# Float32 fillers and a new order for all 780 tasks of a fused attention and maxout kernel

## The chip, the cores and the metric

One core of a Trainium2 chip runs the whole program. The metric is the device time of one execution in microseconds (us). Of the core's engines, PE (TensorE) does the matrix products, DVE (VectorE), ACT (ScalarE) and POOL (GpSimd) do element-wise work, and SP (SyncE) issues DMAs. Each engine works through its own instructions strictly in the order in which the program lists them, and waits at semaphores for the others.

## The reference

Attention with B=4, H=8, S=768, D=64, followed by a maxout layer:

```python
k_sum = k.reshape(B, H, nb, 32, D).max(axis=3)        # nb = 24 blocks of 32
v_sum = v.reshape(B, H, nb, 32, D).mean(axis=3)
scores_l = scale * q @ k.T                            # kept where |i - j| < 16
scores_s = scale * q @ k_sum.T + log(32)
a = softmax(concat(masked scores_l, scores_s))
attn = a @ concat(v, v_sum)                           # (B, H, S, D)
x = attn.transpose(0, 2, 1, 3).reshape(3072, 512)
out = maximum(x @ w1, x @ w2) @ w_out                 # w1, w2: 512 x 1024; w_out: 1024 x 512
```

All inputs and the output are float32 in HBM.

## The kernel before

**Algebra.** max(h1, h2) = h1 + relu(h2 - h1). So the kernel forms `wd` = w2 - w1 and `w1o` = w1 @ w_out, and computes out = x @ w1o + relu(x @ wd) @ w_out. Products are in bfloat16.

**Work units.** A task is a short run of instructions on one engine. There are 780. Names carry the batch b, the head pair hp (0 to 3, two heads each) and the group grp (0 to 2, 256 query rows each). In order of data flow:

- `load kb·hp`, `load qb·hp`, `load vb·hp`: one DMA each from SP (`load_kq`, `load_v`); `load w0` to `load w3` (two DMAs each: one piece of w1 and of w2) and `load wo0` to `load wo3`. They land in a ring of 13 buffers (`land`).
- `cast k`, `cast q`, `cast v`: float32 to bfloat16, on DVE, ACT or POOL (`copy`, line 593). `turn k`, `turn q`: transpose on PE (line 624), or by DMA (line 628) for the pairs 22, 23, 30 to 33. `place`: out of PSUM. `max k`: block maximum (line 650, DVE). `wrap`, `tails`, `sums k`: the window's neighbours and the block maxima put beside the keys.
- `hide` (a mask product, line 690, batch 0 only), `scores` (line 701), `exp` (ACT, line 715), `mask` (DVE, line 725, batches 1 to 3), `values` (lines 757 and 762), `inv` and `x` (DVE, lines 813 and 816), then `xt`: x transposed, on PE plus a copy for batch 0 (lines 831 and 593), by a DMA of SP for the others (line 822).
- `odd v`, `sums`, `all sums`: v shifted by 64 rows, and the block means of v copied where `values` reads them.
- `wd 0` to `wd 3` (line 856): w2 - w1, on DVE or POOL; `w1b`, `turn w1`, `w1t`: w1 transposed for `w1o` (line 897).
- `hidden b·grp·n` (line 913, eight 128x256 products each, n = 0 to 3), `relu` (lines 922 and 924), and `out b·grp·u` (first part line 940, two more parts line 947), `copy out` and `store` (line 958). `hidden` with n odd reads wd 1 and wd 3; with n even it reads wd 0 and wd 2.
- `warm` (line 982): products that nobody reads, into a free PSUM bank; 14 of them fill PE's time while the first loads arrive. Each is two 128x512 bfloat16 products of the constant `identity`, which a DVE copy makes (line 328) from the float32 constant `ident32` of POOL.

**What sets the order.** `Plan.given` takes three lists of the constant `CFG` and does no planning: `order` (the task numbers in program order), `engines` (a letter for each task: T for PE, D, A, P, S) and `slots` (which buffer of its ring each new tile takes). The prices handed to `op` are therefore not used at run time. PSUM is one ring of eight banks; a task that takes a bank waits for the last reader of what was in it.

**Batches overlap.** PE works on `hidden` and `out` of one batch between the pieces of the next batch's attention. In batch 0 there is no earlier batch, so until `wd` is there PE has only the attention of batch 0 and the fillers.

Of the kernel before, what the change touches and what calls it, by code (L numbers as in the profile page):

```python
# [56 lines left out]
""".split()))  # L57
CFG["engines"] = "".join("""
PDPPPDDDPAPDPDDDDPTTTTTTTTTTTTTTSSSAAAATDDPPSSSADPATAAPPSSSPDDPTADDDSSSPDDPTADDPSSDPTASSPATDSSDATDSSPATASDSASASDDTDTAD
PPPDDTDTADPDADDTATDDPDDDPTATDDPPDDTTATDDTDTTATDDTDTTATDDTDTTATDDTDTTATDDTATTATDDTDSSSPSSSPSSSDSSSPPADAPDDDTAPDPAAPDPAT  # L60
DTDDADDDPTATDDPADDTADTDDSTADTDDSTADTDDSATPTADADADDTDTDDADAATADTDDSTADTDDSTADTDDSSSSPSSSASSSASSSPPDAPDDPPTDPPPAAAPPATDT
ADPAAAATPTADPPPDTADTDDSTADTDDSTADTDDSPSPSDDPAAASASDDPPPTADTDDSTADTDDSTADTDDSSSSPSSSPSSSASSSPPDAPDDPDTAPADPPPPPASPSDDAD
PDSDSDDPPDTADTDDSTADTDDSTADTDDSASPSADAADPSDSADAPDTADTDDSTADTDDSTADTDDSTTATTATTDTTDTDTATDTATTTDSTTTDSTATATATATTTAATTTAS
TATATDTDTTTASTTTDSTDTATDTDTTTDATTTDSTDTATATDTTTDATTTASTATDTATATTTDSTTTDSTATDTATATTTDATTTAATDTATATATTTASTTTASTATATATATT
TDSTTTAATDTDTDTDTTTDSTTTDATDTATDTDTTTDATTTASTATDTDTATTTAATTTDSTTTDSTTTAA
""".split())
# [58 lines left out]
class Task:  # L125
    NEVER = 10 ** 9
    done, start = NEVER, None
# [107 lines left out]
def kernel(  # L235
# [39 lines left out]
    def bank(buf, n=512, dt=F32, second=0):  # L275
        a = bank_tile[:, buf.ap + second]
        return (a if dt is F32 else a.bitcast(BF16))[:, 0:n]
# [782 lines left out]
```

## Time and profile before

| | |
|---|---|
| runs | 167.3, 166.43, 167.31 us (median 167.3) |
| profiled execution | 166.2 us, its span 164.4 us |
| PE busy | 153.0 us of the span (93%) |
| DVE, ACT, POOL busy | 113.0, 92.9, 57.8 us |
| `warm` products | 28, 8.7 us of PE's busy time |
| HBM | 25.17 MB read, 6.29 MB written |

The span runs from the first to the last instruction of the program; the execution's own time is 1.8 us longer. Rows of the timeline give the start, the length, the engine, the line, output and inputs, and how many instructions were merged; in square brackets stands the idle time of the engine before them and what ended it. A matmul's recorded end is modelled and holds some 0.16 us of pipeline after its last column, so the pace of PE is read from start to start. Some matmul records are missing.

### The profile page before, as it was taken

What the parts mean: (1) busy time and instruction counts of PE and PEld (TensorE: products, weight loads), DVE (VectorE), ACT (ScalarE), POOL (GpSimd) and SP (SyncE); (2) the same over time, 40 slices, a digit from 0 to 9 for tenths busy, and PEclk for the clock granted to TensorE, in tenths of its full rate; (3) what the DMA queues carried; (4) which work ended last, traced back from release to release, by engine and by line L of the source; (5) the groups of instructions that cost most, each with busy time, mean ns of one, the idle gap of its engine ahead of it and who ended that gap; (6) DMA issues with size and microseconds to landing.
All of it is one profiled execution on the core that took longest, in us unless ns stands there. A gap on an engine that the chain in (4) does not pass through costs nothing.

```text
span 164.4 us, 4431 instructions
## 1 busy us (share of the span) xinstructions
PE 153.0 (93%) x1793; PEld 100.2 (61%) x1812; DVE 113.0 (69%) x224; ACT 92.9 (57%) x134; POOL 57.8 (35%) x91
## 2 busy tenths in 40 slices
PE   5889978999999999999999999999899999999992
PEld 2346657998565644575687646678545467766651
DVE  3698898579856899994989986569746654163221
ACT  3469995794577698836996645283937312012010
POOL 6058757302242385534672546034630000000000
PEclk9999999999999999999999999999999999999999
DMA  5999999999999999999979997997999996311015
GB/s 157 289 331 303 273 386 383 383 382 371 274 190 289 271 233 219 130 232 136 201 169 229 228 209 162 121 261 150 220 245 335 319 174 167 58 64 70 0 66 189
DMA packets 67700, 36.46 MB, mean 222 GB/s; under 512 B 54624, under 2 KB 61664, under 8 KB 67680
## 3 DMA queue, kind: packets, MB, share of 16 engines
q1 hardware_dynamic: 66208, 33.76, 87.6%
q10 hardware_dynamic: 1472, 2.43, 4.4%
q8 instruction: 14, 0.23, 0.6%
q14 instruction: 6, 0.05, 0.1%
HBM read 25.17 MB, written 6.29 MB: 191 GB/s over the span
## 4 chain that ended last, share of the span: by engine, by line
PE 62%; DMA 14%; DVE 11%; issue 4%; SPq 4%; ACT 2%; POOL 1%; ACTq 0%; POOLq 0%; DVEq 0%
PE banks L913 19%; PE banks L947 17%; PE banks L940 10%; DMA land<-in_k_dram 8%; DMA out_dram<-o 6%; PE banks L897 4%; PE banks L624 3%; PE banks L757 3%; DVE vx L593 3%; PE banks L701 2%; PE banks L982 2%; DVE ks L650 2%; DVE pb L725 2%; DVE kqb L593 1%; SPq L428 1%
## 5 line engine op out<-in xcount | busy, mean ns | idle before, releaser
L913 PE MATMUL banks<-xt,wd 128*128 128x256 bf16 x384 | 45.9, 273 | 0.1
L947 PE MATMUL banks<-wo,g 128*128 128x512 bf16 (+2 forms) x194 | 43.4, 362 | 1.8 <-issue 1.6
L913 PEld LDWEIGHTS <-wd 128*128 128x128 bf16 x384 | 37.3, 98 | 7.8 <-issue 0.5
L947 PEld LDWEIGHTS <-g 128*128 128x128 bf16 x208 | 18.7, 98 | 17.3
L715 ACT ACTIVATE pb<-banks 128x1024 bf16<-128x1024 f32 x24 | 23.6, 1026 | 6.2 <-PE banks L701 3.8
L940 PE MATMUL banks<-w1o,xt 128*128 128x512 bf16 (+2 forms) x100 | 23.5, 362 | 0.2
L922 ACT ACTIVATE g<-banks 128x512 bf16<-128x512 f32 x27 | 15.2, 604 | 7.6 <-PE banks L913 7.6
L924 DVE TENSOR_SCALAR g<-banks 128x512 bf16<-128x512 f32 x21 | 14.1, 686 | 7.8 <-PE banks L913 7.6
L816 DVE TENSOR_TENSOR xs<-banks,inv 128x512 bf16<-128x512 f32 x24 | 16.0, 686 | 4.9 <-DMA xt<-xs 4.4
L593 POOL COPY vx<-sums 32x792 bf16<-32x792 bf16 x15 | 14.7, 983 | 12.5 <-ACT sums L593 7.0
L725 DVE TENSOR_TENSOR pb<-pb,mask 128x1024 bf16<-128x1024 bf16 (+1 forms) x24 | 16.4, 710 | 4.0 <-ACT pb L715 3.7
L593 ACT COPY o<-banks 128x512 f32<-128x512 f32 (+1 forms) x8 | 4.4, 546 | 25.6 <-PE banks L947 21.1
L593 POOL CAST kqb<-land 128x768 bf16<-128x768 f32 x9 | 8.9, 985 | 20.1 <-DMA land<-in_q_dram 9.8
L940 PEld LDWEIGHTS <-xt 128*128 128x128 bf16 x104 | 9.9, 98 | 9.4
L650 DVE TENSOR_REDUCE ks<-kx 128x24 bf16<-128x768 bf16 x16 | 15.0, 945 | 0.2
L593 DVE COPY o<-banks 128x512 f32<-128x512 f32 (+2 forms) x10 | 6.2, 621 | 10.2 <-PE banks L947 8.7
L593 POOL CAST vx<-land 128x768 bf16<-128x768 f32 x10 | 8.9, 889 | 10.2 <-DMA land<-in_v_dram 10.2
L593 ACT CAST kqb<-land 128x768 bf16<-128x768 f32 x11 | 10.3, 943 | 3.2 <-DMA land<-in_k_dram 2.5
L593 DVE CAST kqb<-land 128x768 bf16<-128x768 f32 x12 | 7.0, 590 | 7.1 <-DMA land<-in_k_dram 4.7
L624 PE MATMUL banks<-ident,kqb 128*128 128x128 f32 x60 | 9.7, 278 | 1.4 <-DVE kqb L593 1.1
L757 PEld LDWEIGHTS <-pb 128*64 128x64 bf16 (+1 forms) x384 | 8.0, 110 | 4.9 <-issue 2.8
L757 PE MATMUL banks<-vx,pb 128*64 128x65 bf16 (+1 forms) x384 | 9.5, 196 | 1.3 <-DVE xs L816 0.8
(87 smaller groups left out, 183.1 us busy)
## 6 DMA issues: line engine op xcount, KB each, us to landing
land<-in_k_dram SPq DMA_DIRECT2D x16, 384.0 KB, 6.0
land<-in_v_dram SPq DMA_DIRECT2D x16, 384.0 KB, 6.9
land<-in_q_dram SPq DMA_DIRECT2D x16, 384.0 KB, 5.9
land<-in_moe_w_dram SPq DMA_DIRECT2D x8, 512.0 KB, 9.6
land<-in_moe_w_out_dram SPq DMA_DIRECT2D x4, 512.0 KB, 10.0
out_dram<-o SPq DMA_DIRECT2D x7, 256.0 KB, 4.0
out_dram<-o ACTq DMA_DIRECT2D x4, 256.0 KB, 2.8
out_dram<-w1t SPq DMA_DIRECT2D x3, 256.0 KB, 3.4
```

The lines of the kernel that those rows point to most:

```text
L593: {"D": nc.vector.tensor_copy, "A": nc.scalar.copy, "P": nc.gpsimd.tensor_copy}[e](out=o, in_=i)
L624: nc.tensor.transpose(out=bank(ps)[:, 128 * j:128 * j + 128], in_=src.ap[:].bitcast(F32)[:, 128 * j:128 * j + 128], identity=ident32[:])
L650: op("D", 0.95, lambda e: nc.vector.tensor_reduce(out=ks.ap[:, 0:nb], in_=free(kt(), 128, [256, NM], [192, 2], [32, 2], [1, 32]), axis=AX. ...
L715: op("A", {"A": 1.03}, lambda e: nc.scalar.activation(out=spread(pb.ap[:, 0, 0:1], [192, 8], [128, 2], [1, 64]) if PW > 128 else spread(pb ...
L725: nc.vector.tensor_tensor(out=o, in0=o, in1=spread(mask[:, 2 * u:2 * u + 1, 0:1], [0, n], [64, 2], [1, 64]), op=ALU.mult)
L757: nc.tensor.matmul(out=o, lhsT=p[r], rhs=vx[b].ap[r, par, hp + n, 2 * grp + u, a, 0:D + 1], start=(PW == 128 or par == 0), stop=(last and ...
L816: op("D", 0.69, lambda e: nc.vector.tensor_tensor(out=x.ap[:].rearrange("p n u a d -> p n (u a) d"), in0=spread(bank_tile[:, ps.ap, 0:1], ...
L913: nc.tensor.matmul(out=bank(ps)[:, 256 * s:256 * s + 256], lhsT=wd_tile[:, quarter, c, 128 * s:128 * s + 128], rhs=x.ap[:, c, :], start=(c ...
L922: nc.scalar.activation(out=o, in_=bank(ps), func=ACT.Relu)
L924: nc.vector.tensor_scalar_max(out=o, in0=bank(ps), scalar1=0.0)
L940: nc.tensor.matmul(out=bank(ps, c1 - c0), lhsT=x.ap[:, c, sl], rhs=w1o[c].ap[:, cols], start=(c == 0), stop=False)
L947: nc.tensor.matmul(out=bank(ps, c1 - c0), lhsT=g.ap[:, f, sl], rhs=wo[f // 2].ap[:, f % 2, cols], start=False, stop=(f == FC - 1))
```

## The change

1. A filler becomes one 128x256 float32 product of `ident32`.
2. `order`, `engines` and `slots` are replaced as a whole. The tasks and what they compute stay the same, 185 of the 780 change their engine, and nearly all change their place.
3. One price of the planner (ACT's cast) is 1.0 instead of 1.06; nothing at run time reads it.

```diff
 CFG["order"] = list(map(int, """
-44 32 2 0 3 10 12 1 4 6 11 15 13 8 112 20 30 26 56 25 46 113 116 9 122 7 123 126 14 47 16 117 34 118 132 168 28 23 133
...
+44 22 20 26 19 0 5 10 3 9 32 4 56 1 6 11 12 13 112 34 18 113 132 122 116 118 7 15 117 45 46 68 14 33 31 133 123 27 25
...
 CFG["engines"] = "".join("""
-PDPPPDDDPAPDPDDDDPTTTTTTTTTTTTTTSSSAAAATDDPPSSSADPATAAPPSSSPDDPTADDDSSSPDDPTADDPSSDPTASSPATDSSDATDSSPATASDSASASDDTDTAD
...
+PDPDDPPPDDPPDPPPPPTTTTTTTTTTTTTTSSSPPADTDAPDSSSADADTDDDDSSSPDDDTADDDSSSPDPPTAADDSSPPTASSPATDSSDATASSPATDSPSPSDSDATDTDD
...
 CFG["slots"] = list(map(int, """
-0 1 0 0 0 0 0 0 0 0 0 0 1 0 2 1 3 0 0 0 1 1 1 0 0 0 0 0 4 0 0 2 4 0 0 0 1 5 2 0 0 0 0 0 2 0 0 1 4 1 0 1 4 1 0 0 0 0 0
...
+0 0 1 0 1 0 0 0 0 1 2 0 0 0 0 0 3 0 0 1 2 0 0 0 0 0 4 5 6 0 0 1 1 2 0 3 1 0 0 0 0 0 0 0 0 1 0 1 0 2 4 0 2 3 6 0 3 0 0
...
-            copy(eng, {"D": 0.58, "A": 0.84 if by_dma else 1.06, "P": 0.83 if by_dma else 1.05}, cast, by_engine=True,
+            copy(eng, {"D": 0.58, "A": 0.84 if by_dma else 1.0, "P": 0.83 if by_dma else 1.05}, cast, by_engine=True,
...
-            for _ in range(2):
-                nc.tensor.matmul(out=bank(ps), lhsT=identity[:], rhs=spread(identity[:, 0:1], [0, 4], [1, 128]),
-                                 start=True, stop=True)
+            nc.tensor.matmul(out=bank(ps, 256), lhsT=ident32[:], rhs=spread(ident32[:, 0:1], [0, 2], [1, 128]),
+                             start=True, stop=True)
```

The lists read out, for the stretches that matter below ("x2" is a repeat):

| list | before | after |
|---|---|---|
| PE, up to the first `hidden` | warm x4, turn k00, k01, hide 001, warm x2, turn k02, warm x3, sums 02, warm x3, sums 00, warm, turn q01 ... turn w1 1, x000, x001, x020, x021, k12, then hidden 023 | warm x5, turn k00, warm, turn k02, k01, warm x4, hide 001, turn q01, sums 00, warm, sums 02, warm, turn q00, warm, turn k03, scores 001, warm ... turn w1 3, x020, x001, w1 1, then hidden 003 |
| PE, up to the first `hidden` with n even | hidden 023, 003, 021, turn w1 2, hidden 011, turn w1 0, turn k10, hidden 013, 001, then 022 | hidden 003, 001, turn x021, k12, hidden 023, 013, turn w1 0, hidden 011, 021, turn k10, turn w1 2, then 002 |
| SP, weights | w3 x2, w1 x2, k12, w2, w0, k10, w0, w2, wo1, k13, k11, wo0, wo2, wo3 | w3 x2, w1 x2, k12, k10, w0 x2, w2 x2, wo0, k11, wo1, wo2, k13, wo3 |
| engine of wd 0, 1, 2, 3 | DVE, POOL, DVE, POOL | POOL, POOL, DVE, POOL |
| PE, batch 1 into 2 | ... scores 100, values 102, 101, out ... hidden 113, 110, 111, 112, out x3, turn q20, hidden 120, out x2, scores 201, 200 | ... scores 100, out x2, turn q21, out, values 101, 102, out ... hidden 112, 110, 111, 113, out x2, turn q20, out, scores 201, 200 |
| cast q20; sums k20 | DVE; ACT | POOL; POOL, right behind cast q20 |
| SP, batch 2 into 3 | xt 200, turn k32, xt 220, turn k33, load k31, xt 221, xt 201, load q32, store 000, xt 202 ... | xt 200, turn k32, xt 220, xt 201, xt 221, turn k33, load q32, turn k30, xt 202 ... (load k31 before xt 200; store 000 on ACT) |
| PE, batch 2 into 3 | ... hidden 201, 203, out x2, hidden 200, 212, 210, 211, 202, out, hidden 213, 220 ... scores 320, 321 | ... hidden 200, 201, 202, 211, 213, out, hidden 203, out, hidden 210, out x2, hidden 212, 220 ... scores 320, 321 |
| copy out on DVE, ACT | 15, 11 | 7, 19 |
| all sums on DVE, ACT, POOL | 6, 6, 20 | 15, 8, 9 |

More of the change, by code (lines that the diff above doesn't have):

```diff
@@ L30 @@
 CFG["order"] = list(map(int, """
[26 rows of a table removed]
[26 rows of a table added]
 """.split()))
 CFG["engines"] = "".join("""
-PDPPPDDDPAPDPDDDDPTTTTTTTTTTTTTTSSSAAAATDDPPSSSADPATAAPPSSSPDDPTADDDSSSPDDPTADDPSSDPTASSPATDSSDATDSSPATASDSASASDDTDTAD
[L60 to L65, printed above, removed]
+PDPDDPPPDDPPDPPPPPTTTTTTTTTTTTTTSSSPPADTDAPDSSSADADTDDDDSSSPDDDTADDDSSSPDPPTAADDSSPPTASSPATDSSDATASSPATDSPSPSDSDATDTDD
+APPDPTPTADDDDDDTATDDADPDATPTADAAADTTATDDTATTATDDTDTTATDDTATTATDDTDTTATDDTDTTATDDTASSSASSSPSSSDSSSDPDADDDDPTAAPDPDADAAT
+PTADAPDAATDTADDDPDTADTDDSTADTDDSTADTDDSPTPTDDAPPDATDTADAAPATADTDDSTADTDDSTADTDDSSSSDSSSASSSPSSSAPAPPPDPPTAAPDAPADPDTPT
+ADDAPDATATDDPAPATADTDDSTADTDDSTADTDDSDSDSDDDPPPSDSDDPDATADTDDSTADTDDSTADTDDSSSSASSSASSSASSSPDDPPDDDPTADDDPAPAPPSPSDDDD
+PASDSADDPPTADTDDSTADTDDSTADTDDSDSASADDADPSASADPDDTADTDDSTADTDDSTADTDDSTTDTTATTDTTATDTATDTDTTTDATTTASTATDTDTDTTTASTTTAS
+TDTDTATDTTTAATTTASTATATDTDTTTAATTTDSTATATATATTTASTTTAATATDTDTATTTASTTTASTATDTDTATTTASTTTASTDTDTDTATTTDSTTTASTATDTATATT
+TAATTTDATATATDTDTTTASTTTDSTATATATDTTTAATTTAATATATATDTTTASTTTASTTTDSTTTDA
 """.split())
 CFG["slots"] = list(map(int, """
[11 rows of a table removed]
[11 rows of a table added]
 """.split()))
```

70 rows, old and new, of the table turn are left out of this document.

## Prediction

> **What bounds the kernel now.** I read the page first (PE is busiest), then the busy time by stretches.
>
> ```profile
> 0.00:28.00 28.00, 23.00 (x353) 14.07 (x354) 21.76 (x62) 18.90 (x27) 17.69 (x36) 1.00 1.04 301
> 28.00:50.00 22.00, 21.83 (x223) 16.66 (x225) 16.00 (x27) 15.19 (x25) 5.82 (x8) 1.00 1.05 320
> 50.00:75.00 25.00, 24.27 (x312) 14.71 (x314) 21.87 (x42) 18.73 (x24) 12.57 (x20) 1.00 1.09 221
> 75.00:100.00 25.00, 24.53 (x341) 15.85 (x348) 20.24 (x33) 17.89 (x25) 12.54 (x17) 1.00 1.02 198
> 100.00:130.00 30.00, 28.53 (x333) 18.57 (x327) 20.35 (x40) 17.93 (x27) 9.16 (x12) 1.00 1.06 226
> 130.00:164.40 34.40, 30.89 (x256) 20.29 (x257) 12.81 (x23) 4.25 (x9) 0.00 (x0) 1.00 0.45 109
> ```
>
> The columns are the stretch, its length, busy time of PE, its weight loads, DVE, ACT and POOL, then the granted clock (1.00 is full). From 28 us on PE is the bound: it idles 0.17, 0.73, 0.47 and 1.47 us in the four stretches up to 130. The last has 3.51, nearly all of it behind PE's end at 161.15, which the last row of PE's timeline gives:
>
> ```profile
> 159.88 1.27 PE L947 MATMUL banks<-wo,g 128*128 128x256 bf16 x16
> ```
>
> So 0.26 us of it is idle before that end, and 28 to 161 holds 3.10 in all. Part of that is no time at all. The waits say:
>
> ```profile
> PE banks L947 <- issue: 1.6, 10, 0.2
> ```
>
> ```profile
> 66.43 0.81 PE L947 MATMUL banks<-wo,g 128*128 128x512 bf16 x3 [0.16 <-issue]
> ```
>
> An `out` part has four products; here three are listed, the first one's record is missing, and its time counts as idle. Ten such gaps make 1.6 us. True idle from 28 us on is 3.10 - 1.6 = 1.5 us. A new order can win that and what it gains in the head, nothing else: the products stay the same.
>
> The head has two gates, both set by DMA. Timeline rows of POOL, PE, DVE and PE:
>
> ```profile
> 25.49 2.36 POOL L856 TENSOR_TENSOR wd<-land,land 128x1024 bf16<-128x1024 f32 x1 [0.18 <-DMA land<-in_k_dram]
> ```
>
> ```profile
> 29.11 2.78 PE L913 MATMUL banks<-xt,wd 128*128 128x256 bf16 x24
> ...
> 33.83 4.53 PE L913 MATMUL banks<-xt,wd 128*128 128x256 bf16 x40
> ```
>
> ```profile
> 32.77 2.52 DVE L856 TENSOR_TENSOR wd<-land,land 128x1024 bf16<-128x1024 f32 x2 [1.90 <-DMA land<-in_moe_w_dram]
> ```
>
> wd 1 ends at 25.49 + 2.36 = 27.85; only then can a `hidden` with n odd run. wd 0 and wd 2 (both in the last row, 1.23 each) end at 32.77 + 2.52 = 35.29; only then one with n even. The run of 40 products starts with `hidden` 013 and 001, so 022, the first with n even, starts at 33.83 + 2 x 0.87 = 35.57 (a `hidden` is 8 x 0.109 = 0.87 us, 4.37 for 40 in the chain row below). PE is thus only 0.28 us behind the second gate.
>
> **The change, part by part.** *Fillers.* Rows of the chain of waits, then of PE and DVE:
>
> ```profile
> 12.68 0.43 PE banks L982 x2
> 13.11 0.34 PE banks L624 x3
> ...
> 33.99 4.37 PE banks L913 x40
> ```
>
> ```profile
> 1.86 3.54 PE L982 MATMUL banks<-identity 128*128 128x512 bf16 x8 [1.86 <-DVE identity L328]
> ```
>
> ```profile
> 1.35 0.46 DVE L328 CAST identity<-ident 128x128 bf16<-128x128 f32 x1 [1.35 <-POOL ident masks.py:199]
> ...
> 5.14 1.09 DVE L593 CAST kqb<-land 128x768 bf16<-128x768 f32 x2 [1.95 <-DMA land<-in_k_dram]
> ```
>
> A filler takes 0.43 us now. The nearest float32 row, the turn, has 0.34 / 3 = 0.113 for 128 columns, so 0.23 for 256; the upper end is today's 0.43. I take 0.23, as the row of the same type: 14 fillers need 3.2 instead of 6.0 us. None of it is on the path: PE idles 5.0 us before 28 as it is, and casts release the turns. If that cover went, the two ends are 14 x 0.2 = 2.8 us apart. They start some 0.46 us earlier, since they read `ident32` and no longer wait for the DVE copy; the first real product still waits for k at 5.14, so that is worth 0. The first eight products ran at 3.54 / 8 = 0.44 each, twice the later 0.22, though the granted clock reads full. The Trainium skill, "FP8 and Floating Point Precision", TensorE Precision Notes, says that true float32 takes four passes through the array. By it a filler would be 4 x 0.109 = 0.44, as long as today's, and the sum would be the same; no row here shows a float32 product that isn't a transpose.
>
> *Head up to the first gate.* PE's first `hidden` is now 003, ahead of `turn` x021 and k12. It needs wd 1, xt 000 (ACT) and xt 020 (DVE). POOL: the loads up to w1 are the same twelve plus four, so wd 1 ends at 27.85 again; POOL's longer list before it (`amean`, `apart` and two casts more) fits into its idle time, 10.3 of the first 28 us. ACT and DVE from rows:
>
> ```profile
> 12.02 1.05 POOL L593 CAST kqb<-land 128x768 bf16<-128x768 f32 x1 [1.09 <-DMA land<-in_k_dram]
> ```
>
> ```profile
> L715 ACT ACTIVATE pb<-banks 128x1024 bf16<-128x1024 f32 x24 | 23.6, 1026 | 6.2 <-PE banks L701 3.8
> ```
>
> ```profile
> L816 DVE TENSOR_TENSOR xs<-banks,inv 128x512 bf16<-128x512 f32 x24 | 16.0, 686 | 4.9 <-DMA xt<-xs 4.4
> ```
>
> ```profile
> L650 DVE TENSOR_REDUCE ks<-kx 128x24 bf16<-128x768 bf16 x16 | 15.0, 945 | 0.2
> ```
>
> k03 lands at 12.0. From its cast to xt 000, ACT has 21 tasks: 6 exp at 1.03, two casts and two w1b at about 1.0, 11 smaller ones, 15 us in all. It ends at 27 or later. DVE has 48 tasks from its cast of k02, at about 6.3 us, to xt 020: 4 maxima at 0.95, 5 x at 0.69, 6 places, 2 casts, 31 short copies, 20.5 us. It ends at 26.8 plus waits, and one is plain: q01 is now cast on POOL, behind cast v00 and both `amean` steps, done by about 10.7, and DVE's place of q01 stands behind it for some 1.3 us. So 28.1. I put 003 at 28.1 to 29.
>
> *Between the gates.* Six `hidden` with n odd, two turns of w1, three small turns: 7.0 us. With 003 at 28.1 PE reaches hidden 002 at 35.1, and waits for wd 2, which DVE still makes and whose load still ends the same list of eight: 35.3. With 003 at 29 it is 36.0. Against 35.57 that is -0.28 to +0.4; I take 0.0, the middle. wd 0 moves to POOL (2.36 instead of 1.23), but both halves of w0 now land before w2; started at the latest at 32.77, as now, it ends at 35.1, hidden behind wd 2; uncovered it would cost 1.1. DVE then stands at `wo 2` and `wo 3` for their loads with relu 021 and 012 behind; PE needs the bank of 021 only at `w1o` 2, some 9 us after the gate. 0, and 1 us if that cover goes.
>
> *Batch 1 into 2.*
>
> ```profile
> 65.84 3.59 SPq L822 DMA_TRANSPOSE xt<-xs  x2
> ...
> 70.09 0.48 SPq L428 DMA_DIRECT2D land<-in_q_dram  x1
> ```
>
> ```profile
> land<-in_q_dram SPq DMA_DIRECT2D x16, 384.0 KB, 5.9
> ```
>
> ```profile
> 77.90 0.52 PE L624 MATMUL banks<-ident,kqb 128*128 128x128 f32 x3
> ```
>
> ```profile
> L822 SPq DMA_TRANSPOSE xt<-xs x18: 1188/1264/2510, 65.8 to 139.5; - x18
> ```
>
> ```profile
> L593 POOL CAST kqb<-land x9: 817/991/1364, 12.0 to 118.5; 128x768 bf16<-128x768 f32 x9
> ```
>
> The turn of q20 (77.90) moves one `out` part ahead, to 77.0. q20 lands at about 70.1 + 5.9 = 76.0, and POOL's cast (0.99) ends at 77.0: just in time. But SP issues that load behind xt 101, whose `values` moves one part back on PE (0.86). If all of that arrives, the stall is 0.9 to 1.1 us; if the issue of xt 101 takes the median 1.26 us rather than the 2.1 it seems to take inside the 3.59, it is 0.1. POOL's `sums k20` follows the cast, for `scores` 201. I take 0.3, nearer the median row. Bounds 0 and 1.1.
>
> *Batch 2 into 3.*
>
> ```profile
> 98.22 1.24 SPq L628 DMA_TRANSPOSE kt<-kqb  x1
> 99.51 0.57 SPq L428 DMA_DIRECT2D land<-in_k_dram  x1
> 100.18 3.79 SPq L822 DMA_TRANSPOSE xt<-xs  x2
> ```
>
> ```profile
> 105.48 4.98 PE L913 MATMUL banks<-xt,wd 128*128 128x256 bf16 x40
> ```
>
> ```profile
> 116.59 0.41 PE L701 MATMUL banks<-kt,kx 64*128 64x64 bf16 x16 [0.31 <-ACT g L922]
> ```
>
> ```profile
> 123.35 0.42 PE L701 MATMUL banks<-kt,kx 64*128 64x64 bf16 x19 [0.29 <-ACT o L593]
> ```
>
> Here lies the true idle: 1.47 less four lost records (0.64) is 0.83. The run of 40 takes 4.98 against 4.53 before: it waits within, for xt 221 and 201. These two now go ahead of turn k33 and load k31, so 1.8 us sooner, but hidden 211 moves up three tasks. The two waits for ACT come from a relu and a copy out ahead of `scores`; in the new order ACT takes 19 copies out instead of 11, and DVE 23 relus instead of 21, so they may shift rather than go. I take -0.5 of the 0.83, because the SP step is certain and the ACT ones aren't; bounds -0.83 and +0.5.
>
> *Tail.* PE ends with the same pieces; stores of 301 and 321 are on SP ahead of the last. 0.
>
> Sum: 0.0 + 0.3 - 0.5 = -0.2. The profiled execution took 166.2 (span 164.4), so 166.0; the median of the runs lies 1.1 above it, so 167.1 against 167.3.
>
> **The rivals.** *Faster.* The order wins the idle time: -0.83 in 100 to 130, -0.28 at the gate, -0.3 elsewhere: 165.9; all 1.5 and the gate would be 165.5. For it speaks DVE's load (eight copies out fewer); against it, that the gate caps the head.
>
> *Slower by the head.* There is no cover behind the gates: each us that 003 starts after 28.55 (35.57 - 7.0) is lost. DVE's chain of 48 has no slack, and port conflicts lengthen it:
>
> ```profile
> 22.08 0.93 DVE L593 COPY vx<-apart 32x528 bf16<-32x528 bf16 x2
> ```
>
> Two copies of 0.29 took 0.93 here, beside a POOL copy: 0.35 each time, and more of these copies now run on DVE. The Trainium skill, "SBUF — State Buffer", SBUF: two separate sides, states why: DVE and GpSimd hold a shared port pair exclusively for a whole instruction. Four such conflicts (1.4) and 0.4 more of waits put 003 at 29.9: +1.35 on the sum, 168.4. It decides from 29.6 on.
>
> *Slower by q20.* q20 lands at 77.7, POOL's cast ends at 78.7 and PE stands 1.7 us; with the -0.5 of the next stretch that is 168.5. It decides from a landing at 77.4 on. Against it: only one part separates the two orders.
>
> *Fillers don't fill.* At 0.23 they leave PE idle, the doubled pace of the first eight products lasts longer, and the eight turns of the head double: 8 x 0.34 = 2.7 us more, of which I put a third on the path: 168.0.
>
> **How the numbers follow.** About 0.5% (0.84 us) is what a measurement of this kernel can tell from no change. My forecast, within it: 0.37. Faster 0.29, slower by the head 0.16, by q20 0.12, by fillers 0.06. So faster 0.29, same 0.37, slower 0.34. The time is 167.1, the forecast's own range 166.5 to 168.1. The whole range, 165.4 to 169.3, reaches from all true idle won to a late head and a late q20 in part together.
>
> **What would show it.** Right: first `hidden` row at 28 to 29; the wd row that ends last still at 35.2 to 35.4, PE's first n-even `hidden` right behind; xt 201 landed before PE asks; PE's idle in 100 to 130 below 1.2. Wrong: `hidden` after 29.6, a PE wait over 1 us before `turn` q20 or `scores` 201, an n-even `hidden` before 35 (then the gate isn't the DMA's), or waits spread over 50 to 130 that I did not look for.

## The result and the profile after

| | before | after |
|---|---|---|
| runs, us | 167.3, 166.43, 167.31, 169.51 (median 167.31) | 171.09, 174.67, 172.48, 174.41 (median 173.44) |
| ratio to before, 95% interval | | 1.030, 1.020 to 1.040 |
| profiled execution, its span | 166.2, 164.4 | 171.09, 169.3 |

The change is 3% slower (6.1 us in the medians, 4.9 us in the profiled spans). The ratios here and below leave out executions over 1.5% above the fastest of their kernel (here 169.51, 174.67 and 174.41); the medians hold them. The forecast was 167.1 with a range to 169.3: wrong in size and side. On the chips of the experiments the kernel before ran in 165.1 to 165.8 us and the change, run again, in 173.12: 1.043 (1.034 to 1.052).

Busy time by stretch in the changed kernel, with the columns of the first fence of the prediction:

```profile
0.00:28.00 28.00, 21.20 (x272) 15.04 (x273) 20.28 (x46) 17.81 (x26) 17.61 (x42) 0.98 1.02 292
28.00:50.00 22.00, 21.98 (x233) 17.62 (x233) 16.70 (x30) 12.99 (x21) 12.27 (x13) 0.95 1.05 325
50.00:75.00 25.00, 25.00 (x354) 14.30 (x353) 21.32 (x45) 20.01 (x28) 8.09 (x13) 1.00 0.89 191
75.00:100.00 25.00, 24.72 (x315) 16.79 (x314) 19.07 (x34) 18.92 (x27) 11.24 (x15) 1.00 1.16 210
100.00:130.00 30.00, 28.16 (x331) 18.21 (x331) 21.65 (x44) 18.25 (x25) 8.14 (x12) 1.00 1.07 200
```

PE has been busy 1.8 us less by 28 us (21.20 against 23.00), and the granted clock is below 1.00 in the first two rows. From 28 to 100 PE idles even less than before: 0.02, 0 and 0.28 us. In 100 to 130 it idles 1.84 against 1.47. PE's waits in the changed kernel (us in total, times, longest) say for whom:

```profile
PE banks L913 <- DMA xt<-xs: 3.0, 2, 1.8
PE banks L757 <- DVE vx L593: 2.6, 3, 1.8
```

**The head.** Rows of PE, DVE and POOL in the changed kernel:

```profile
27.06 1.23 PE L757 MATMUL banks<-vx,pb 128*64 128x65 bf16 x25 [1.78 <-DVE vx L593]
...
32.03 1.91 PE L913 MATMUL banks<-xt,wd 128*128 128x256 bf16 x16
...
39.05 3.22 PE L913 MATMUL banks<-xt,wd 128*128 128x256 bf16 x28
```

```profile
11.66 0.56 DVE L593 COPY qx<-banks 128x768 bf16<-128x768 bf16 x1 [1.44 <-PE banks L624]
...
18.99 1.90 DVE L593 COPY vx<-apart 32x528 bf16<-32x528 bf16 x3
...
24.10 2.90 DVE L593 COPY vx<-apart 32x528 bf16<-32x528 bf16 x3
...
37.66 1.21 DVE L856 TENSOR_TENSOR wd<-land,land 128x1024 bf16<-128x1024 f32 x1
```

```profile
24.51 2.34 POOL L856 TENSOR_TENSOR wd<-land,land 128x1024 bf16<-128x1024 f32 x1 [3.47 <-issue]
27.17 2.36 POOL L856 TENSOR_TENSOR wd<-land,land 128x1024 bf16<-128x1024 f32 x1 [0.32 <-DMA land<-in_moe_w_dram]
```

The first `hidden` (003) starts at 32.03, 2.9 us after the first of before (29.11). The first with n even (002) starts at 39.05 instead of 35.57: 3.5 us. Of DVE's two groups of three copies (a single one takes 0.29), the one at 19 us loses 1.0 us, the one at 24 us 2.0. In the second the third copy ends at 27.00, just behind POOL's wd 3 (24.51 + 2.34 = 26.85). `values` waits for it. In the group at 19 us the second and third copy took 0.81 and 0.74 and ended 0.15 us behind a cast and a copy of POOL. In the kernel before, DVE had products `x` beside wd 3, which read PSUM and weren't held (two in 1.29):

```profile
22.94 2.36 POOL L856 TENSOR_TENSOR wd<-land,land 128x1024 bf16<-128x1024 f32 x1
```

```profile
23.36 1.29 DVE L816 TENSOR_TENSOR xs<-banks,inv 128x512 bf16<-128x512 f32 x2
```

**The two later stalls.** Rows of PE in the changed kernel:

```profile
107.09 3.11 PE L913 MATMUL banks<-xt,wd 128*128 128x256 bf16 x27 [1.83 <-DMA xt<-xs]
```

```profile
139.26 1.92 PE L913 MATMUL banks<-xt,wd 128*128 128x256 bf16 x16 [1.12 <-DMA xt<-xs]
```

The first is hidden 200, which ran two products at 104.88 and then waited for xt 220. That landed at 99.5 before and at 107.1 now: SP issued it at 101.46, behind the loads of q33 and k31 and turn k32, and not at 96.91. Rows of SP, before and then changed (in the last row xt 220 is the first of three):

```profile
96.91 1.22 SPq L822 DMA_TRANSPOSE xt<-xs  x1
```

```profile
95.73 1.53 SPq L428 DMA_DIRECT2D land<-in_k_dram  x1
97.37 1.55 SPq L822 DMA_TRANSPOSE xt<-xs  x1
99.02 2.34 SPq L628 DMA_TRANSPOSE kt<-kqb  x1
101.46 5.01 SPq L822 DMA_TRANSPOSE xt<-xs  x3
```

It also took 5.6 us from its issue to its landing, against 2.6. The second stall is hidden 311, waiting for xt 301.

### The profile page after: what moved, and what is told of

The parts are those of the page before. It is cut to its first block, busy times and chain, and to the rows that moved or that the text cites. A ratio compares the mean times of both kernels' runs of the same rounds, so it can differ in the third digit from the quotient of the medians.

```text
span 169.3 us, 4460 instructions
## 1 busy us (share of the span) xinstructions
PE 156.3 (92%) x1812; PEld 104.2 (62%) x1812; DVE 109.6 (65%) x216; ACT 98.8 (58%) x141; POOL 57.3 (34%) x92
## 4 chain that ended last, share of the span: by engine, by line
PE 66%; DMA 15%; DVE 10%; SPq 2%; issue 2%; POOL 1%; ACT 1%; DVEq 0%; POOLq 0%
PE banks L913 20%; PE banks L947 18%; PE banks L940 11%; DMA xt<-xs 5%; DMA kt<-kqb 5%; PE banks L897 4%; PE banks L624 4%; DVE vx L593 4%; DMA land<-in_q_dram 3%; PE banks L701 3%; PE banks L757 3%; DMA land<-in_k_dram 2%; SPq L822 1%; DVE kx L593 1%; DVE xs L816 1%
## 5 line engine op out<-in xcount | busy, mean ns | idle before, releaser
L947 PE MATMUL banks<-wo,g 128*128 128x512 bf16 (+2 forms) x208 | 47.0, 363 | 0.0
L924 DVE TENSOR_SCALAR g<-banks 128x512 bf16<-128x512 f32 x23 | 15.4, 686 | 20.2 <-PE banks L913 20.0
L593 POOL CAST kqb<-land 128x768 bf16<-128x768 f32 x11 | 10.5, 959 | 25.7 <-DMA land<-in_q_dram 13.2
L725 DVE TENSOR_TENSOR pb<-pb,mask 128x1024 bf16<-128x1024 bf16 (+1 forms) x24 | 14.4, 627 | 2.5 <-ACT pb L715 2.4
L593 ACT COPY o<-banks 128x512 f32<-128x512 f32 (+1 forms) x11 | 6.3, 569 | 16.0 <-PE banks L947 13.8
L757 PE MATMUL banks<-vx,pb 128*64 128x65 bf16 (+1 forms) x384 | 10.7, 203 | 2.7 <-DVE vx L593 2.6
L981 PE MATMUL banks<-ident 128*128 128x256 f32 x28 | 9.7, 484 | 1.4 <-POOL ident masks.py:199 1.4
L624 PEld LDWEIGHTS banks<-ident,kqb 128*128 128x128 f32 x60 | 7.1, 143 | 6.3 <-DVE kqb L593 2.0
L593 POOL COPY vx<-sums 32x792 bf16<-32x792 bf16 x8 | 7.9, 988 | 8.5 <-ACT sums L593 8.2
L593 POOL CAST vx<-land 128x768 bf16<-128x768 f32 x6 | 5.9, 983 | 10.4 <-DMA land<-in_v_dram 10.3
```

Of the source, the lines that this page charges most:

```text
L593: {"D": nc.vector.tensor_copy, "A": nc.scalar.copy, "P": nc.gpsimd.tensor_copy}[e](out=o, in_=i)
L624: nc.tensor.transpose(out=bank(ps)[:, 128 * j:128 * j + 128], in_=src.ap[:].bitcast(F32)[:, 128 * j:128 * j + 128], identity=ident32[:])
L725: nc.vector.tensor_tensor(out=o, in0=o, in1=spread(mask[:, 2 * u:2 * u + 1, 0:1], [0, n], [64, 2], [1, 64]), op=ALU.mult)
L757: nc.tensor.matmul(out=o, lhsT=p[r], rhs=vx[b].ap[r, par, hp + n, 2 * grp + u, a, 0:D + 1], start=(PW == 128 or par == 0), stop=(last and ...
L924: nc.vector.tensor_scalar_max(out=o, in0=bank(ps), scalar1=0.0)
L947: nc.tensor.matmul(out=bank(ps, c1 - c0), lhsT=g.ap[:, f, sl], rhs=wo[f // 2].ap[:, f % 2, cols], start=False, stop=(f == FC - 1))
```

## The experiments

Theory A: the new order of the head makes the loss, with two waits for xt added later. Theory F: the float32 fillers make it. Theory P within A: DVE's copies stand while POOL runs. (The first expectations call F "Theory B".) Kernels that share a chip share the runs of the kernel before; ratios are to those.

### Which part of the change costs

The changed kernel with the old head: every task before the old cut (226 places in the old list) in the old order, with its old engine and buffer.

```diff
-order, engines, slots of the change, all 780
+order, engines, slots of before for the first 226 tasks, of the change for the rest
```

> The changed kernel with the head of the kernel before: the order, engines and buffers of every task up to the first hidden tiles (about the first 36 us) are those of before, everything later and the float32 fillers are those of the change. Theory A (the head's order is most of the loss): the first hidden tile starts at 29.1 +- 0.4 us instead of 32.0, the first tile of an even number at 35.6 +- 0.4 instead of 39.0, the dip of the granted clock at 25 to 30 us (0.69) is gone, and the time is 173.4 - 3.5 = 169.9 us or, if the dip also makes the spread of the runs, down to 167.5. Theory B (the float32 fillers and the clock they bring make the loss): the fillers are still there, so the time stays at 172 to 174.

Measured: 171.15 (168.81 to 173.56) against 165.61, ratio 1.028 (1.015 to 1.041). The trace is of an execution of 173.56 us. In it the first `hidden` came at 32.8, not 29.1. Two things held it. The first transposes ran at a slower pace than before. PE by form from 5 to 12 us (busy, mean ns), the kernel before and then this one:

```profile
L624 PE MATMUL banks<-ident,kqb 128*128 128x128 f32 x9 | 1.5, 288 | 1.1 <-DVE kqb L593 1.1
```

```profile
L624 PE MATMUL banks<-ident,kqb 128*128 128x128 f32 x9 | 2.4, 427 | 0.6 <-DVE kqb L593 0.6
```

And PE stood 1.90 and 1.78 us for nothing that the profile shows ("issue"); more on that in the last section.

The reverse, the kernel before with the new head and its own fillers:

```diff
-order, engines, slots of before, all 780
+order, engines, slots of the change for the first 219 tasks, of before for the rest
```

> The kernel before with the head of the change (order, engines and buffers of the tasks up to the first hidden tiles), with its own two bfloat16 matmuls as a filler and its own order later. Theory A: first hidden tile at 32.0 +- 0.5 us, first of an even number at 39.0 +- 0.6, time 167.3 + 3.5 = 170.8, up to 173 with the clock's dip. Theory B: 167.3 +- 0.8, since no float32 filler is in it.

Measured: 172.00 against 165.61, 1.042 (1.034 to 1.050); first `hidden` at 32.8, first with n even at 39.8. The head alone costs as much as the whole change. Of the 5.7 us by which PE ends later in its trace than before, 4.7 are there at `hidden` 000 (52.90 against 48.16), and 1.2 are two waits for DVE, 0.41 and 0.75 us at 71 and 75 us, which the change doesn't have.

Only the filler, and only the filler undone:

```diff
-for _ in range(2): matmul(bank(ps), identity, ... 128x512 bf16)
+matmul(bank(ps, 256), ident32, ... 128x256 f32)
```

> The kernel before with one line changed: a filler is one float32 matmul of 256 columns. Theory F (in the old head the float32 fillers leave PE at its slow pace longer: with the old head and these fillers the first transposes took 427 ns each instead of 288): transposes of the keys at the slow pace until about 10 us, scores 002 at 18 instead of 16, first hidden tile 2 to 3.7 us later than before, time 165.6 + 2 to 3.5 = 167.6 to 169 where before stands at 165.6. Theory A alone (a filler only fills): ratio to before 1.000 +- 0.004.

> The changed kernel with the two bfloat16 matmuls of before as a filler, all else as changed. Theory A (order): 1.03 to 1.04 of before, as the change, since the new order itself keeps PE waiting. Theory F (fillers are the whole loss): 1.00 to 1.01.

Measured: in the old order 168.31 against 165.14, 1.015 (1.007 to 1.024); the change with bfloat16 fillers 172.86, 1.042 (1.034 to 1.051), as with float32. So the fillers aren't the loss of the change. Behind the old head the kernel with them is slower, but not by the slow pace that theory F named. PE by form from 5 to 12 us, the old order with float32 fillers:

```profile
L624 PE MATMUL banks<-ident,kqb 128*128 128x128 f32 x9 | 1.6, 291 | 1.3 <-DVE kqb L593 1.3
```

291 ns is the old pace; the 427 of the first kernel was that execution's own. (The trace of the last kernel below, which has the old head and bfloat16 fillers, shows 418.) This trace is of an execution of 166.71 us, the shortest of four. Its first `hidden` is 1.1 us late (30.17), behind two stands of PE of 0.92 and 1.43 us for nothing that the profile shows. Whether the fillers have a part in that, and where the others lose more, stays open.

The old head and the old fillers, the new order only later:

```diff
-order, engines, slots of before after the first 226 tasks
+those of the change
```

> The changed kernel with the head of before and the fillers of before: only the order, engines and buffers after about 36 us are new. Theory A: the first hidden tile at 29.1 +- 0.5, and what is left is the later order's own difference, which the traces put at 4.9 - 3.5 = 1.4 us: ratio 1.005 to 1.012. Theory F without A: ratio 1.00. If the later order alone costs more, 1.02 and over.

Measured: 168.53 against 165.14, 1.021 (1.012 to 1.029). So this kernel loses about half as much. The parts don't add up: 4.2% and 2.1% make 4.3% together. The traces say why in part: the 1.2 us of waits above are of neither order alone, and of the 1.4 us by which this kernel's span (165.8) is longer than before, 0.6 lie in the head that it didn't change (first `hidden` at 29.71, behind stands of 0.98 and 1.48 us). The change itself on such a chip:

```diff
(no edit)
```

> The changed kernel itself once more, as the measure for the kernels beside it on the same chip: ratio to before 1.030 to 1.042; first hidden tile at 32.0 to 32.8 us, DVE's copies at 24 us 2.4 to 2.9 us for three.

Measured: 173.12 against 165.78, 1.043 (1.034 to 1.052).

### What holds the copies on DVE

wd 3 cut to 8 of 256 columns:

```diff
-out=wd_tile[...], in0=landed(fs[1], ...), in1=landed(fs[0], ...)
+the same, each with [:, :, :, 0:8 if n == 3 else 256]; a memset of wd 3's place on POOL ahead of cast q03
```

> The changed kernel with wd 3 on POOL cut to 8 of its 256 columns per row (the rest of that weight difference is zero, so the hidden tiles of n = 3 and 1 are computed from a part of the weights); one clear of it goes into POOL's idle stretch at 13 us. Theory P (the three DVE copies of apart into vx at 24.1 took 2.90 us instead of 0.9 because POOL's wd 3 holds the way to the memory): the three copies take 0.9 to 1.1 us, the values behind them start 2 us earlier, the first hidden tile is at 30.0 instead of 32.0, and the ratio falls by 0.012, to 1.02. Rival (the copies are slow for another reason, such as DMA traffic): 2.5 us or more for the three, ratio as the change, 1.03.

Measured: 173.27, 1.046 (1.039 to 1.054). No gain, and the copies weren't faster: both as the rival had it. The rows show that it was POOL even so. DVE and POOL in its profile (of an execution of 178.38 us; its lines stand two to four further down):

```profile
20.72 0.93 DVE L595 COPY vx<-apart 32x528 bf16<-32x528 bf16 x3
...
25.98 3.66 DVE L595 COPY vx<-apart 32x528 bf16<-32x528 bf16 x3
```

```profile
22.99 0.25 POOL L860 TENSOR_TENSOR wd<-land,land 128x32 bf16<-128x32 f32 x1 [2.14 <-issue]
26.12 2.36 POOL L860 TENSOR_TENSOR wd<-land,land 128x1024 bf16<-128x1024 f32 x1 [2.88 <-DMA land<-in_k_dram]
28.42 1.06 POOL L595 CAST kqb<-land 128x768 bf16<-128x768 f32 x1
```

With wd 3 out of the way wd 1 started sooner, and the copies stood beside it and the cast behind it until 29.64 (POOL: 29.48). At 20.72, with POOL nearly free, three such copies took 0.93. So the price follows whatever POOL runs. It also follows wd 3 when that moves. DVE and POOL of the change's second run:

```profile
23.41 2.36 DVE L593 COPY vx<-apart 32x528 bf16<-32x528 bf16 x1
...
26.20 0.82 DVE L593 COPY vx<-apart 32x528 bf16<-32x528 bf16 x3
```

```profile
23.27 2.35 POOL L856 TENSOR_TENSOR wd<-land,land 128x1024 bf16<-128x1024 f32 x1 [2.20 <-issue]
```

Here wd 3 began 1.2 us sooner and another copy stood: 2.36 us, to 25.77, where wd 3 ends at 25.62. The three of 24 us now take 0.82. The remedy is to take the copies off DVE:

```diff
-engines: all sums 040, 060, 061 on D
+engines: all sums 040, 060, 061 on P (POOL idles there, ahead of wd 3)
```

> The changed kernel with one choice of engine changed: the copies all sums 040, 060 and 061 go to POOL, which stands idle from 21.0 to 24.5 us, ahead of its wd 3, instead of DVE. Theory P (one DVE copy stood from 24.63 to 27.00 us beside POOL's wd 3, 24.51 to 26.85, and a copy on POOL's own queue can't be held by it): DVE's chain ends 2.9 us sooner (2.0 of standing and 0.9 of work), the first hidden tile comes at 29.5 to 30.3 instead of 32.0, and the time falls by 1.5 to 2.5 us (ratio to the change 0.985 to 0.99). Rival Q (ACT's exponentials, the last of the pair at 25.2 to 26.2 instead of 21.0, hold the tiles by themselves): the first hidden tile gains 1.0 us or less, the time stays within 0.5%.

Measured: the first `hidden` at 30.34 instead of 32.62 beside it, as P said (x 000 ends at 25.0 instead of 28.0). But the time fell only from 173.12 to 171.94 (1.038, 1.031 to 1.045): the intervals overlap. PE by stretch (busy, granted clock):

```profile
135.00:140.00 5.00, 2.92 (x63) 1.00 0.88 233
140.00:145.00 5.00, 5.00 (x25) 0.66 0.38 74
```

PE came sooner to hidden 311, stood 2.08 us for xt 301, and then ran 5 us at a clock of 0.66: 1.7 us more. The change beside it waited 1.34 us there and kept its clock. So 0.7 + 1.7 = 2.4 us, about as much as the head won, went there.

Undoing the four moves from POOL to DVE instead:

```diff
-engines: all sums 001, 020, 021, 061 on D
+engines: all sums 001, 020, 021, 061 on P
```

> The changed kernel with four choices of engine undone: all sums 001, 020, 021 and 061 on POOL as before, in the changed order. Theory P: DVE's group of 1.90 us at 19.0 us goes, its 040 and 060 come before POOL's wd 3 begins, the first hidden tile comes at 29.5 to 30.5 and the time falls by 1.5 to 2.5 us (0.985 to 0.99 of the change). Rival R (POOL pays what DVE saves: 2.5 us more on POOL push the casts of v02 and v03 back, and with them the last values): first hidden tile at 31.5 or later, time within 0.5% of the change or above.

Measured: 173.79, 1.050 (1.040 to 1.060), first `hidden` at 32.6: rival R. The casts of v02 and v03 came later, and another copy stood beside wd 3 (23.96 + 2.49 = 26.45):

```profile
24.28 2.40 DVE L593 COPY vx<-vx 64x768 bf16<-64x768 bf16 x1
```

### The clock's dip

Fillers in PE's wait of the head:

```diff
 PE: ...
+warm, values 002 ...
-values 000, values 022
+values 000, warm x4, values 022
```

> The changed kernel with five fillers more: four in PE's order ahead of values 022, where PE then waits 1.78 us, and one ahead of values 002. They compute nothing that is used. Theory G (PE's clock is granted at half for some 3.4 us after a stretch in which PE idled about 2 us, here 0.50 from 27.5 to 30 us, and that costs 1.7 us of the 3.5 the head lost): the granted clock stays 1.00 from 20 to 35 us, the values after the wait run at full pace, the first hidden tile comes 0.7 to 1.7 us sooner (31 to 31.6 where the change has 32.0 to 32.6), the time falls by 0.7 to 1.7 us (0.99 to 0.996 of the change). Rival N (the dip doesn't come from PE's idling, or costs nothing because DVE sets the pace): the dip stays, or the time stays within 0.3%.

The granted clock of the change, in 2.5 us stretches:

```profile
22.50:25.00 2.50, 1.79 (x71) 1.00 1.02 388
25.00:27.50 2.50, 0.72 (x34) 0.89 1.06 394
27.50:30.00 2.50, 2.40 (x67) 0.50 1.05 386
30.00:32.50 2.50, 2.50 (x47) 0.93 1.05 386
```

(0.11 + 0.50 + 0.07) x 2.5 = 1.7 us of pace, or 3.4 us at half clock. With the fillers:

```profile
25.00:30.00 5.00, 4.76 (x117) 1.00 1.06 389
30.00:35.00 5.00, 4.42 (x56) 1.00 1.05 384
```

The dip is gone, so PE's idling made it. But the first `hidden` came at 32.2, between the 32.0 and 32.6 of the change's two traces: DVE's chain sets that time, and the half pace lay in its shadow. Time 174.91, 1.040 (1.023 to 1.057): the same. Its trace has another wait for xt 301 (3.4 us) and a dip behind that. There no other engine covers it, and it costs in full.

### The two waits for xt

Moved in SP's queue:

```diff
 SP:
-load q33, load k31, xt 200, turn k32, xt 220, xt 201, xt 221
+load q33, xt 200, turn k32, xt 220, xt 201, xt 221, load k31
-xt 321, xt 320, xt 301
+xt 321, xt 301, xt 320
```

> The changed kernel with two moves in SP's queue alone: the load of k31 goes behind xt 221 (as it stood before), and xt 301 goes ahead of xt 320. Theory A (the two later stalls of PE are transfers of xt that queue behind these): the stall of 1.83 us at 105 and that of 1.12 us at 138 go, 171 to 170.5 in the median, and the profiled execution 2.5 to 3 us shorter at the same clock. Theory C (something else arrives just as late, so a wait takes the place of each): the time stays within 0.5 us of the change and PE waits as long at the next task.

> Both edits together: the head of the kernel before on the changed kernel, and the two moves in SP's queue. Theory A: 169.9 - 2.9 = 167.0 or, without the dip's spread, 164.6 to 165.5, so 1 to 2.5 us faster than the kernel before. Theory C: 167 to 168.5, no better than before. Theory B: 172 or more.

Measured: 182.06, 1.105 (1.096 to 1.114), and with the old head 179.09, 1.083 (1.072 to 1.094). Both theories missed. ACT in the first of them:

```profile
115.44 0.83 ACT L593 CAST kqb<-land 128x768 bf16<-128x768 f32 x1 [9.72 <-DMA land<-in_k_dram]
```

The cast of k31 kept its place on ACT and waited 9.72 us for a load that now came 12 us later. Behind it lay what PE needed: PE stood 6.5 us at 110. Its clock dipped after that too.

Moved in PE's order instead:

```diff
 PE:
-out 101, out 100, hidden 200, 201, 202, 211, 213, out 101, hidden 203, out 201, hidden 210, out 121
+out 101, out 100, out 101, out 121, hidden 200, 201, 202, 211, 213, 203, out 201, hidden 210
-out 210, hidden 311, 313, out 311, out 221
+out 210, out 221, hidden 311, 313, out 311
```

> The changed kernel with three moves in PE's order alone: the second out 101 and out 121 go ahead of hidden 200, and out 221 ahead of hidden 311. Theory A (PE's stalls of 1.83 us at 105 and 1.12 us at 138 are the order's: ready work stands behind the waiting tile): both fall to 0.3 us or less, the time falls by 1.7 to 2.7 us (0.985 to 0.99 of the change). Theory C (a wait takes the place of each, as it did where a load was moved): the time stays within 0.5% of the change.

Measured: 175.95, 1.060 (1.050 to 1.069). The first wait went: hidden 200 ran through. The second grew (the trace is of an execution of 177.34 us):

```profile
143.40 3.60 PE L913 MATMUL banks<-xt,wd 128*128 128x256 bf16 x16 [3.38 <-DMA xt<-xs]
```

xt 301 landed 5.9 us after its issue (3.5 in the change); the trace doesn't show why. As a trial xt 301 went ahead and the stores behind it, with the copies on POOL:

```diff
 engines: all sums 040, 060, 061 on P, SP:
-store 101, store 110, store 120, store 121, xt 321, xt 320, xt 301
+store 101, xt 321, xt 301, xt 320, store 121, store 120, store 110
```

> The changed kernel with the three sums copies on POOL (first hidden tile at 30.3 instead of 32.6, which alone gave only 0.5% since PE then stood 2.08 us at 137 us for xt 301 and its clock fell to 0.66 for the next 5 us), and in SP's queue xt 301 ahead of xt 320 and the stores 110, 120 and 121 behind both. Theory G: xt 301 lands 1.5 us sooner or more, PE's wait there is under 1 us, the clock stays 1.00 behind it, and the time falls by 2.3 + 1 + 1.7, to 168 to 169.5 (ratio to before 1.015 to 1.025). Rival S (the stores or the transposes moved back collide later): ratio 1.035 or more.

The same with PE's three moves, and SP's and PE's moves behind the old head and fillers:

> As the last, and also the second out 101 and out 121 ahead of hidden 200 and out 221 ahead of hidden 311 in PE's order. If the head's held copies, the two waits for xt and the clock's dips after them are the whole loss: 173.1 - 2.3 - 1.8 - 2 - 1.7 = 165.3 (ratio to before 0.995 to 1.01). If something else is left: 1.015 or more, and PE's waits name it.

> The head and the fillers of before, the later order of the change (1.021 of before, with two waits for xt of 1.1 us each), and in it the same moves in SP's queue and in PE's order. If those waits are what the later order costs: 168.5 - 2.2 = 166.3 or less, ratio 0.995 to 1.008. If its length comes from other places: 1.015 to 1.02.

Measured: 173.09, 1.038 (1.025 to 1.051); 170.96, 1.031 (1.018 to 1.044); 170.47, 1.016 (1.001 to 1.031). xt 301 landed 4.9 and 4.1 us sooner than in the change and, in the third, 2.2 sooner than without the moves, and yet PE stood 2.1, 2.8 and 2.8 us at the same place. DVE and PE of the second:

```profile
139.18 0.69 DVE L816 TENSOR_TENSOR xs<-banks,inv 128x512 bf16<-128x512 f32 x1 [3.86 <-DMA xt<-xs]
```

```profile
139.93 1.91 PE L913 MATMUL banks<-xt,wd 128*128 128x256 bf16 x16 [2.77 <-DVE xs L816]
```

DVE's x 322 waited for a buffer of xs that xt 320, now last, had not read, and hidden 311 for the bank that x 322 empties. So xt 320 went back to its place:

```diff
 SP:
-store 101, store 110, store 120, store 121, xt 321, xt 320, xt 301
+xt 321, xt 320, xt 301, store 101, store 110, store 120, store 121
```

> The changed kernel with the three sums copies on POOL, the moves of out 101, out 121 and out 221 in PE's order, and in SP's queue the stores 101, 110, 120 and 121 behind xt 301, with xt 320 left ahead of xt 301 (in the last kernel xt 320 stood behind it, DVE's x 322 waited 3.86 us for xt 320 to empty its buffer of xs, and PE's hidden 311 2.77 us for x 322 to empty its bank). If a late transfer of xt is all that holds PE at 138 us: no wait over 0.7 us there, 170.9 - 2.5 = 168.4 (ratio to before 1.012 to 1.02), and what is left over before is the head's 2 us. If yet another wait takes its place: 1.025 or more.

> The head and fillers of before, the later order of the change, and the same moves in PE's order and SP's queue. With a wait of 2.77 us at 138 us it stood at 1.016; without it 1.000 to 1.006 of before, which would make the later order's cost the two waits for xt alone. At 1.012 or more the later order costs elsewhere as well.

Measured: 171.25, 1.030 (1.025 to 1.035), and behind the old head 169.00, 1.012 (1.005 to 1.019). A third wait took the place, the same in both. PE of the first:

```profile
137.41 0.32 PE L757 MATMUL banks<-vx,pb 128*64 128x65 bf16 x8 [1.87 <-ACT o L593]
```

The stores now behind xt 301 hold the output buffers that ACT's copy out needs (it waited 4.81 us for one), and with them a bank of PE. All repairs together bring the change from 1.043 to 1.030 and its later order from 1.021 to 1.012; none of the kernels beats the one before. What the later order costs by itself isn't closed. The trace of the last kernel (of an execution of 170.51 us) has a span 4.3 us longer than before (168.7), but 3.9 of it are there at the first `hidden` (32.99), in a head that is the same task for task. So some of the 1.012, and of the 1.021 without the repairs, may be the head's and not the later order's.

## Why the prediction was wrong

- *Head up to the first gate: the step that failed, by size.* It added DVE's 48 tasks at their free durations and one wait for q01 (1.3; measured 1.44) and put 003 at 28.1 to 29. Added were 1.0 and 2.0 us in which DVE's copies stood beside POOL. DVE's three other waits of some length (0.38, 0.23 and 0.39 us) add 1.0: 28.1 + 3.0 + 1.0 = 32.1; x 020 ended at 30.51, its copy into xt at 31.98, and 003 started at 32.03. The prediction had the mechanism as its rival "slower by the head", with four conflicts of 0.35. But a conflict doesn't cost 0.35: it costs what is left of POOL's operation, and that was wd 3 with 2.34. The row it was taken from held the rule already: its two copies didn't take 0.35 more each, but 0.29 and 0.71, and the second ended 0.15 us behind the POOL copy of 0.74. It should have asked which POOL operation runs beside which DVE copy: at 24 us both lists had one.
- *Between the gates.* 7.0 us from 003 to 002, "no cover": 39.05 - 32.03 = 7.02. Right, so the whole lateness reached the gate: taken 0.0, measured +3.5. The DMA's gate no longer set the time: w2 had landed, but wd 2 started only at 37.66, behind DVE's relus. The 35.3 was off too: w2 landed at 34.77 instead of 33.97, so an early head would have met that gate at about 36.0.
- *wd 0 to POOL.* At 0: no wait for it shows. wd 1 was put at 27.85 again and ended at 29.53, as w1 landed later; 003 came later still.
- *Fillers.* Taken as 0.23 us, measured as 0.43: a filler leaves two records, and eight records take (PE, changed kernel)

```profile
8.05 1.89 PE L981 MATMUL banks<-ident 128*128 128x256 f32 x8
```

so 1.89 less some 0.16 of pipeline, by four fillers, is 0.43: the upper bound. The rule of four passes (the Trainium skill, "FP8 and Floating Point Precision", TensorE Precision Notes), set aside there, agrees with that row. Cost on the path in the new order: 0, as forecast (1.043 with float32, 1.042 with bfloat16). In the old order the kernel with them was 1.5% slower.
- *Batch 1 into 2.* Taken 0.3 (0 to 1.1). PE, changed kernel:

```profile
80.47 0.55 PE L624 MATMUL banks<-ident,kqb 128*128 128x128 f32 x3 [0.15 <-POOL kqb L593]
```

  0.15 us. Right.
- *Batch 2 into 3: wrong in sign.* Taken -0.5 (to +0.5), because xt 221 and 201 go ahead of load k31. They did, and didn't matter: with hidden 200 first, xt 220 is what PE waits for, and it stands behind load k31, which had moved ahead of xt 200. The list of the change said so ("load k31 before xt 200"); the working priced only the two transfers that had waited before. 1.83 us of waiting took the place of the 0.83 of true idle: +1.0 instead of -0.5.
- *Tail.* Taken 0; the wait for xt 301 was 1.12 there, and 2.08 to 3.4 in kernels with the same order there.
- *Chances.* The head as a loss had 0.16 and was priced at 168.4 by the small conflicts. "003 after 29.6" and "waits that I did not look for" were the signs named for being wrong; the first decided it.

The sum by measured terms is 3.5 + 0.15 + 1.0 + 1.1 = 5.8; the spans differ by 4.9. Three points up to which PE has done the same tasks in both orders, and its end, show where the lateness arose: 3.5 us at `hidden` 000 (51.63 against 48.16), 3.15 at `sums` 2 (73.60 against 70.45), 3.9 at `values` 301 (133.14 against 129.21), 5.2 at PE's end. The last store follows 0.3 us sooner than before. So the head makes most of it, and 0.6 us are won back in places that no term had.

Shown by runs: the new head alone costs the whole (1.042); DVE's copies stand for POOL's operation (they followed wd 3 to another copy when it began sooner, and gave 2.3 us at the first `hidden` when moved to POOL, though at most 1.2 us of the time). Shown by traces only: the two waits for xt. Open: what the later order costs by itself (1.012 with all repairs), what float32 fillers cost behind the old head, and how much of the change's time the clock's later dips make.

## What to carry to other kernels

An engine's chain is not the sum of its free durations: list what POOL runs beside each SBUF-to-SBUF copy of DVE, and price a meeting at what is left of POOL's operation. Where a gate has no cover, each wait on the chain ahead of it arrives in full; name the last transfer that each moved task needs in the new order, not the one that it needed in the old. In a kernel whose orders are all tight, moving one transfer, store or load finds the next buffer: here three of the repairs made a new wait each. And before a part of a kernel is charged with a difference, see in the trace whether the difference lies in a stretch that this part doesn't touch.

## What the runs showed of the hardware

- **A DVE copy waits for the whole POOL operation.** 2.36 and 2.37 us for a copy of 0.29, 2.40 for one of 0.36, each ending 0.15 to 0.25 us behind POOL. `x` of DVE, which reads PSUM, took its 0.69 beside wd 3 in the kernel before. The Trainium skill, "SBUF — State Buffer", SBUF: two separate sides, says that the loser blocks for the full instruction; the traces agree.
- **PE's clock halves after a wait, but not always.** 3.4 us at half clock cost 1.7 us where PE sets the pace (2.08 us of waiting, 0.66 over the next 5 us) and 0.4 at most in DVE's shadow (first `hidden` at 32.6 without the fillers, 32.2 with them). A wait of 2.77 us at the same place in another kernel (the change with the copies on POOL and PE's and SP's moves) left it at 1.00, and the wait of 1.9 us in the last two kernels brought a fall in the first (0.85 and 0.81 in the 5 us stretches from 135 us) and none in the second. Rows of the wait of 2.77:

```profile
135.00:140.00 5.00, 2.23 (x31) 1.00 0.90 285
140.00:145.00 5.00, 5.00 (x39) 1.00 0.57 164
```

  The Trainium skill, "TensorE: Matmul & The Clock Gate", Part 1: The HAM clock gate, tells of a free-running window of 3413 ns: the length of 3.4 us fits it. It has the clock fall after at least one idle window of that length; here a wait of 2.08 us was enough, and the measurement decides.
- **PE stands at fixed places of its program.** Behind its records 223 and 351, so 128 products and 128 weight loads apart, PE stood for nothing that the profile shows, at one of the two or both in every trace but that of the short wd 3. Counts by stretch and rows of PE, of the kernel with the old head and fillers and the later order of the change:

```profile
0.00:22.00 22.00, 18.42 (x223) 1.00 1.03 274
0.00:28.50 28.50, 22.99 (x351) 1.00 1.04 301
```

```profile
22.66 0.44 PE L757 MATMUL banks<-vx,pb 128*64 128x65 bf16 x15 [0.98 <-issue]
...
28.87 0.68 PE L831 MATMUL banks<-identity,xs 128*128 128x128 bf16 x9 [1.48 <-issue]
```

  In another kernel with that head they were 2.24 and 1.75 us, in the profile of before 0.66 at the second place alone. The change shows the first (0.71); with the copies on POOL the second shows (0.48 to 1.57), and takes part of what they win. The Trainium skill, "Runtime: NRT & Kernel Launch", Instruction fetch mechanics, has code loaded in blocks of 256 instructions and calls the cost of a boundary mostly hidden: the spacing agrees, the cost doesn't, while loads run at some 380 GB/s. The traces record this loading as packets of 16 KiB on a queue of its own:

```profile
q8 instruction: 14, 0.23, 0.6%
```

  Wherever PE stood at one of the two places, it went on 1.26 to 1.54 us behind the end of the first or second packet: here 21.23 to 22.66 and 27.54 to 28.87, in that other kernel 24.20 to 25.67 and 30.74 to 32.15, in the change 23.34 to 24.67. Where it came to the place over 2 us behind the packet, as in the change at the second one (29.64 to 31.75), it didn't stand. So the traces say that PE waited for its code. No run changed this, and the traces don't show what makes a packet late. It may be much of what separates executions of one kernel.
